# Keys of the first head group by key tiles, another order in the first batch's second pass, and one load of queries moved behind five eighths of w_in

## The chip, the cores and the metric

The kernel runs on one core of a Trainium2 chip. The metric is the time of one execution on the device in microseconds: 383.92 is the median of three runs of the kernel before (383.72 to 384.61).

## What is computed

Sigmoid attention, and a dense layer pair behind it. In float32 the reference is

```
scores = q @ k^T / sqrt(64) - log(448)          # 8 batches, 12 heads, 448 x 64 each
attn   = sigmoid(scores)                        # no softmax
x      = attn @ v, heads side by side           # 3584 tokens x 768
h      = x @ w_in                               # 768 -> 2048
g      = h * sigmoid(beta * h)                  # beta: one number for each of 2048 columns
out    = g @ w_out                              # 2048 -> 768
```

## The kernel before

Everything is multiplied in float16. A batch has three groups of four heads (`QPB` = 3), 24 groups in all. A group is two slots of two heads. The 448 keys of a head are three key tiles of 128 (`jt` 0 to 2) and a last one of 64 (`jt` 3, `JF`); in the raw layout the four blocks of 32 that make up a key tile lie three blocks apart (`(i j) d`, i = 4, j = 3).

**Loads.** POOL issues all loads that cast to float16: queries and keys (`load_one`, L110), values (`load_v`, four loads of 144 KB at L131 and two of 48 KB at L138 for a batch), w_in in eight slices of 256 columns (`load_w_in`, L148), w_out in four (L156). It has eight of them under way: each waits for the one that was issued eight before. SP issues the first group's queries (first half, seven of fourteen blocks) and keys without a cast (L517), as whole float32 rows into `gt`, a tile that is free then, and `beta_in` (L546); later it issues the stores. The order on POOL at the start is: first-half queries and keys of groups 1 and 2, values of batch 0, second-half queries of groups 0, 1 and 2, the eight slices of w_in, queries and keys of group 3, half of w_out, values of batch 1 and so on.

**Transposes.** For group 0, DVE casts the queries (L537), ACT one half of the keys (L539) and DVE the other (L540). DVE transposes queries (L191) and keys (L199 for key tiles 0 to 2 in one instruction, L203 for the last tile).

**The order** of the start is written by hand, under a manual schedule: an engine runs its instructions in the order of the program. The first batch is worked in two passes of 224 queries (`QH`). In the first pass each group has two half visits. The first (`half_visit(g, 0, 0)`) makes the scores of key tiles 0 and 1, the second (`second` = 1) those of tile 2 and of the last one; ACT turns each score tile into attention (L224). Between them PE runs matmuls on zeros (`idle_units`, L533), nine at the very start and then four or two at a time. `attend(g, c0, n)` multiplies attention by values (L279), and DVE copies the result to `xT` (L288). After the first pass comes group 0's second half, in between the attends of the first pass.

Then the fill begins. `fill_units(n)` takes the next n pieces of dense work from a list: for the first 224 tokens sixteen units of the first layer (`dense1`, units 0 to 15; unit dc needs w_in's slice dc // 2), the same for the second 224, with pieces of the second layer between them from the tenth unit on. A unit of the first layer is six matmuls (L166), a sigmoid on ACT (L305) and a product on DVE (L308), which frees its bank; four banks are shared by these units, the attends and the second layer. Around the change the order is

```
        fill_units(4)
        for g in range(1, QPB):
            for second in range(2):
                half_visit(g, QH, second)
                if second:
                    attend(g - 1, QH, QH)
                fill_units(g if second else 2 + g)
        fill_units(1)
        attend(QPB - 1, QH, QH)
```

so units 0 to 3 stand first, 4 to 6 after group 1's first half visit, 7 after its second and attend(0), 8 to 11 after group 2's first, 12 to 14 after its second and attend(1), and 15 after attend(2).

From group 3 on, a planner hands out fill by a budget in microseconds (`M1H_US`, `M2_US` and so on are its costs): after each `visit(g, jt)` it takes units until the budget of that visit is spent. A visit makes the scores of one key tile for the group's two slots and has ACT weigh both.

Of the kernel before, what the change touches and what calls it, by code (L numbers as in the profile page):

```python
# [8 lines left out]
FP32 = mybir.dt.float32  # L9
FP16 = mybir.dt.float16  # L10
# [3 lines left out]
def kernel(  # L14
# [10 lines left out]
    nc = tc.nc  # L25
# [3 lines left out]
    B, H, S, D = q.shape  # L29
    NTOK, DM = out.shape  # L30
    DFF = moe_w_in.shape[1]
    P = 128
    BLK = 32
# [112 lines left out]
    def load_w_in(c: int):  # L146
        n = DFF // WCH
        nc.gpsimd.dma_start(  # L148
            out=w_in16[:, :, c * n : (c + 1) * n],
            in_=moe_w_in[:, c * n : (c + 1) * n].rearrange("(c p) f -> p c f", p=P),  # L150
        )
# [34 lines left out]
    def transpose(g: int, r: int, c0: int = 0, c1: int = NB):  # L186
        raw = raws[g][:, r]
        if r == 0:
            if g not in qT:
                qT[g] = qTp.tile([P, NB * BLK, PAIR], FP16, tag="qT", name="qT")  # L190
            nc.vector.transpose(  # L191
                out=in_order(g // QPB, qT[g][:, c0 * BLK : c1 * BLK]),
                in_=raw[:, c0:c1].rearrange("p c d -> p (c d)").bitcast(FP32),
            )
            return
        kT[g] = kTp.tile([P, S, PAIR], FP16, tag="kT", name="kT")
        to = kT[g].rearrange("p k e -> p (k e)").bitcast(FP32)
        frm = raw.rearrange("p c d -> p (c d)").bitcast(FP32).rearrange("p (c f) -> p c f", c=NB)
        nc.vector.transpose(  # L199
            out=to[:, 0 : JF * P].rearrange("p (j i q) -> p i j q", j=JF, i=HQ),  # L200
            in_=frm[:, 0:NF].rearrange("p (i j) f -> p i j f", j=JF),
        )
        nc.vector.transpose(  # L203
            out=to[:, JF * P :], in_=frm[:, NF:].rearrange("p c f -> p (c f)")
        )

    def score_tile():
# [23 lines left out]
        return at  # L231


    def visit(g: int, jt: int, also=()):
        if jt < JF:
            todo = [(score_tile(), [s]) for s in (2 * g, 2 * g + 1)]
        else:
            todo = [(score_tile(), [2 * h, 2 * h + 1]) for h in (g, *also)]
        for e in range(PAIR):
            for sco, slots in todo:  # L240
                for s in slots:
                    for hh in range(2):
                        score(sco, 0, s, jt, hh, e, 0, S)
        for sco, slots in todo:
            at = weigh(sco, S)
            for s in slots:
                at_tiles[s, jt, 0] = at
# [259 lines left out]
    with tc.manual_schedule():  # L507
        raws[0] = rawp.tile([P, 2, NB, D], FP16, tag="raw", name="raw")
        wide = gt.rearrange("p a b -> p (a b)").bitcast(FP32)
        cut = NH * D  # L510
        early = [(0, 0, NH), (1, 0, NB)]
        staged = {}
        at = 0
        for r, c0, c1 in early:
            staged[r] = wide[:, at : at + (c1 - c0) * D]
            at += (c1 - c0) * D
            nc.sync.dma_start(  # L517
                out=staged[r],
                in_=(q, k)[r][0, 0:HQ].rearrange("h (p c) d -> (h p) (c d)", c=NB)[
                    :, c0 * D : c1 * D  # L520
                ],
            )
        nc.gpsimd.memset(dummy, 0.0)  # L523
        nc.scalar.activation(out=dummy, in_=dummy, func=AF.Sigmoid, bias=0.0, scale=1.0)

# [7 lines left out]
                nc.tensor.matmul(idle, still[:, 0:P], still, start=True, stop=True)  # L533

        idle_units(9)
        raw = raws[0].rearrange("p r c d -> p r (c d)")
        nc.vector.tensor_copy(out=raw[:, 0, 0:cut], in_=staged[0])  # L537
        transpose(0, 0, 0, NH)
        nc.scalar.copy(out=raw[:, 1, cut:], in_=staged[1][:, cut:])  # L539
        nc.vector.tensor_copy(out=raw[:, 1, 0:cut], in_=staged[1][:, 0:cut])  # L540
        transpose(0, 1)
        for g in range(1, QPB):
            load_one(g, 0, 0, NH)
            load_one(g, 1)
        load_v(0)
        nc.sync.dma_start(out=beta_in[0:NDC], in_=moe_beta.rearrange("(c p) -> c p", p=P))  # L546
        for g in range(QPB):
            load_one(g, 0, NH, NB)
        for c in range(WCH):
            load_w_in(c)  # L550
        for g in range(1, QPB):
            transpose(g, 0, 0, NH)
# [10 lines left out]
        half_visit(0, QH, 0)  # L563
        attend(1, 0, QH)
        half_visit(0, QH, 1)
        for g in range(1, QPB):
            transpose(g, 0, NH, NB)
        attend(2, 0, QH, (0,))
        attend(2, 0, QH, (1,))
# [12 lines left out]
        firsts.close()  # L582
        share_psum(ctx, 2, 4)
        fill_units(4)
        for g in range(1, QPB):
            for second in range(2):
                half_visit(g, QH, second)
                if second:
                    attend(g - 1, QH, QH)
                fill_units(g if second else 2 + g)  # L590
        fill_units(1)
        attend(QPB - 1, QH, QH)
        fill_units(1)
        transpose(QPB, 0)
        transpose(QPB, 1)
# [24 lines left out]
        for i, (g, jt, also) in enumerate(visits):  # L620
            if jt == 0:
# [10 lines left out]
                        load_qk(g + 2)  # L632
                if g + 1 < NQUAD and (g + 1) % QPB == 0:
                    load_v((g + 1) // QPB)
            visit(g, jt, also)
            if jt in (1, 2) and QPB < g < NQUAD - 1:
                transpose(g + 1, jt - 1)
            if jt == 2 and g % QPB == 0 and g > QPB:
# [51 lines left out]
```

## Time and profile before

| what | value |
|---|---|
| median of three runs | 383.92 us |
| the profiled execution | 383.76 us |
| its span, first to last instruction | 382.0 us |
| PE busy | 375.9 us, 98% |
| DVE, ACT, POOL busy | 231.8, 229.5, 66.4 us |
| granted clock of PE | 1.00 in all slices |
| keys of group 0, SP's load | 448 KB, 3.3 us to landing |
| first-half queries of group 0, SP's load | 224 KB, 2.7 us to landing |
| one slice of w_in, POOL's load | 384 KB, median 10.7 us to landing |

The span is what the profiler saw between the first and the last instruction; the execution's own time is 1.8 us longer. Sizes of POOL's loads are those of the float16 written; twice as much is read. PE, LDWEIGHTS (PEld), DVE, ACT, POOL and SP are the engines, `L213` is line 213 of the kernel before. Starts in the timeline are microseconds from the first instruction.

### The profile page before, as it was taken

To read this page: it belongs to the slowest core of one execution; us is meant where nothing else is said; L and a number is where in the kernel's file an instruction comes from. 1 tells how busy PE (TensorE), PEld (TensorE's weight loads), DVE (VectorE), ACT (ScalarE), POOL (GpSimd) and SP (SyncE) were. 2 spreads that over 40 slices of the span, in tenths; PEclk is the share of its full clock that TensorE was granted. 3 is DMA by queue.
4 is the path that set the end of the run, shared out by engine and by line. 5 is a ranking of instruction groups with operands and counts; after the bars stand their busy time and mean duration, and the time that the engine had idled before them with its cause. 6 is when DMAs were issued, how large, how long until landed. Compare 5 with 4: busy or idle time off the path is not lost.

```text
span 382.0 us, 8227 instructions
## 1 busy us (share of the span) xinstructions
PE 375.9 (98%) x3415; PEld 199.2 (52%) x3415; DVE 231.8 (61%) x439; ACT 229.5 (60%) x330; POOL 66.4 (17%) x114
## 2 busy tenths in 40 slices
PE   8999999999999999999999999999999999999996
PEld 3478754444654445444554445544456444555563
DVE  3447366775765557555775657665676665655761
ACT  5987856697465786487355782477752787435200
POOL 7833343140110410040110410113100000000000
PEclk9999999999999999999999999999999999999999
DMA  9999999845363930563363750649303300030033
GB/s 165 172 196 204 198 205 209 178 65 59 50 132 83 122 51 2 130 90 32 50 132 84 102 69 2 131 88 118 50 0 84 85 1 2 2 82 0 2 82 125
DMA packets 42405, 34.71 MB, mean 91 GB/s; under 512 B 21872, under 2 KB 38656, under 8 KB 42368
## 3 DMA queue, kind: packets, MB, share of 16 engines
q0 software_dynamic: 36688, 22.47, 43.5%
q1 hardware_dynamic: 5680, 11.71, 11.6%
q8 instruction: 27, 0.44, 0.5%
q14 instruction: 10, 0.08, 0.1%
HBM read 45.62 MB, written 11.01 MB: 148 GB/s over the span
## 4 chain that ended last, share of the span: by engine, by line
PE 92%; DMA 4%; POOL 1%; issue 1%; ACT 0%; DVE 0%; ACTq 0%; POOLq 0%
PE m_ps L166 73%; PE sco L213 10%; PE av_ps L279 9%; DMA w_in<-in_moe_w_in_dram 3%; DMA raw<-in_k_dram 2%; POOL raw L110 1%; POOL w_in L148 1%; ACT attnT L224 0%; ACT sg L305 0%; DVE osb L340 0%; DVE gt L308 0%; POOL dummy L523 0%; ACTq L305 0%; POOLq L674 0%
## 5 line engine op out<-in xcount | busy, mean ns | idle before, releaser
L224 ACT ACTIVATE attnT<-sco 128x896 f16<-128x896 f32 (+1 forms) x171 | 145.2, 902 | 81.1 <-PE sco L213 80.5
L166 PE MATMUL m_ps<-xT,w_in 128*128 128x448 f16 (+2 forms) x1014 | 154.7, 336 | 0.7 <-DMA w_in<-in_moe_w_in_dram 0.5
L308 DVE TENSOR_TENSOR gt<-m_ps,sg 128x448 f16<-128x448 f32 (+1 forms) x144 | 81.4, 572 | 81.6 <-ACT sg L305 78.1
L166 PEld LDWEIGHTS <-w_in 128*128 128x128 f16 (+1 forms) x1014 | 82.8, 101 | 69.3 <-issue 15.1
L305 ACT ACTIVATE sg<-m_ps,beta_sb 128x448 f32<-128x448 f32 (+1 forms) x144 | 84.3, 597 | 36.9 <-PE m_ps L166 29.8
L166 PEld LDWEIGHTS <-sum 128*64 128x64 f16 (+1 forms) x664 | 48.1, 104 | 33.5 <-issue 7.9
L213 PE MATMUL sco<-qT,kT 32*128 32x448 f16 (+3 forms) x864 | 52.0, 341 | 0.7 <-DVE kT L199 0.5
L166 PE MATMUL m_ps<-w_T,sum 128*128 128x384 f16 (+1 forms) x360 | 51.6, 327 | 0.0
L110 POOL DMA_DIRECT2D raw<-in_q_dram x26 | 14.4, 553 | 181.0 <-DVE kT L203 175.5
L428 DVE TENSOR_TENSOR osb<-m_ps,osb 128x384 f32<-128x384 f32 x60 | 33.3, 555 | 18.8 <-PE m_ps L166 16.9
L166 PEld LDWEIGHTS <-gt 128*128 128x128 f16 (+1 forms) x414 | 31.4, 103 | 23.8 <-issue 6.2
L279 PE MATMUL av_ps<-attnT,v 128*64 128x448 f16 (+3 forms) x432 | 40.2, 338 | 0.0
L398 DVE TENSOR_TENSOR sum<-gt 128x1024 f16<-128x1024 f16 x60 | 39.1, 677 | 0.1
L288 DVE CAST xT<-av_ps 128x448 f16<-128x448 f32 (+1 forms) x54 | 28.5, 567 | 15.3 <-PE av_ps L279 14.3
L166 PE MATMUL m_ps<-w_T,gt 128*64 128x384 f16 (+1 forms) x268 | 34.3, 327 | 0.0
L166 PE MATMUL m_ps<-w_out,sum 128*64 128x384 f16 (+1 forms) x304 | 33.8, 327 | 0.0
L279 PEld LDWEIGHTS <-v 128*64 128x64 f16 (+1 forms) x432 | 20.6, 108 | 18.8 <-issue 9.2
L213 PEld LDWEIGHTS <-kT 32*128 32x128 f16 (+1 forms) x864 | 13.7, 96 | 28.6 <-issue 25.7
L166 PE MATMUL m_ps<-w_out,gt 128*128 128x384 f16 (+3 forms) x146 | 22.6, 327 | 0.0
L131 POOL DMA_DIRECT2D v<-in_v_dram x32 | 19.8, 632 | 10.4 <-DMA w_in<-in_moe_w_in_dram 5.6
L191 DVE STREAM_TRANSPOSE qT<-raw 128x448 f32<-128x448 f32 (+1 forms) x27 | 16.6, 616 | 0.4 <-DMA raw<-in_q_dram 0.3
L431 ACT COPY osb<-m_ps 128x384 f32<-128x384 f32 x12 | 5.8, 481 | 16.8 <-PE m_ps L166 16.8
(25 smaller groups left out, 90.1 us busy)
## 6 DMA issues: line engine op xcount, KB each, us to landing
out_dram<-osb SPq DMA_DIRECT2D x98, 96.0 KB, 1.9
raw<-in_k_dram POOLq DMA_DIRECT2D x23, 224.0 KB, 5.3
raw<-in_q_dram POOLq DMA_DIRECT2D x21, 224.0 KB, 3.9
v<-in_v_dram POOLq DMA_DIRECT2D x32, 144.0 KB, 6.5
w_in<-in_moe_w_in_dram POOLq DMA_DIRECT2D x8, 384.0 KB, 10.7
w_out<-in_moe_w_out_dram POOLq DMA_DIRECT2D x4, 768.0 KB, 13.8
v<-in_v_dram POOLq DMA_DIRECT2D x16, 48.0 KB, 5.9
out_dram<-osb SPq DMA_DIRECT2D x2, 384.0 KB, 3.0
```

Of the source, the lines that this page charges most:

```text
L110: nc.gpsimd.dma_start(out=raws[g][:, r, c0:c1].rearrange("p c d -> p (c d)"), in_=(q, k)[r][b, HQ * t : HQ * (t + 1)].rearrange("h (p c) d ...
L131: nc.gpsimd.dma_start(out=vs[b][i * BLK : (i + 1) * BLK, :, 0:JF].rearrange("p h j d -> p h (j d)"), in_=rows[:, :, JF * i * D : JF * (i + ...
L166: nc.tensor.matmul(to[c : c + step], hidden[:, c : c + step], weights, **({} if step == P else {"tile_position": (0, c)}), **flags,)
L191: nc.vector.transpose(out=in_order(g // QPB, qT[g][:, c0 * BLK : c1 * BLK]), in_=raw[:, c0:c1].rearrange("p c d -> p (c d)").bitcast(FP32),)
L213: nc.tensor.matmul(sco[base : base + nk, hh, u0 : u0 + n], kT[g][lo : lo + BLK, jt * P : jt * P + nk, e], qT[g][lo : lo + BLK, c0 : c0 + n ...
L224: nc.scalar.activation(out=at[:, :, 0:n], in_=sco[:, :, 0:n], func=AF.Sigmoid, bias=NEG_LOG_S, scale=MSCALE,)
L279: nc.tensor.matmul(av[hh * D : (hh + 1) * D, 0:n], vs[b][base : base + nk, 2 * (s % NPAIR) + hh, jt], at[base : base + nk, hh, 0:n], start ...
L288: nc.vector.tensor_copy(out=xTs[b][:, s % NPAIR, c0 : c0 + n], in_=av[:, 0:n])
L305: nc.scalar.activation(out=sg[:, 0:n], in_=m1[:, 0:n], func=AF.Sigmoid, bias=0.0, scale=beta_sb[:, dc : dc + 1])
L308: nc.vector.tensor_tensor(out=gt[:, dc, off : off + n], in0=m1[:, 0:n], in1=sg[:, 0:n], op=ALU.mult)
L398: nc.vector.tensor_tensor(out=sums[t, i], in0=x, in1=y, op=op)
L428: nc.vector.tensor_tensor(out=out, in0=in0, in1=in1, op=op)
```

## The change

1. The keys of group 0 come in three loads on SP, behind the queries: key tiles 0 and 1 (per partition four runs of 512 bytes), key tile 2 (four runs of 256 bytes) and the last tile (one run of 512 bytes). Before it was one load with one run of 3584 bytes per partition. ACT casts key tile 1, DVE tile 0; DVE transposes tiles 0 and 1; then DVE casts tile 2 and the last tile, and transposes these two. A new function `transpose_keys(g, j0, j1)` transposes a range of key tiles; for all other groups it is called with the ranges that were used before.
2. The second-half queries of group 2 are loaded behind five of w_in's eight slices, and transposed between the products of units 6 and 7 instead of before attend(2) of the first pass.
3. The second pass of the first batch is written out in another order: attend(0) stands behind group 1's first half visit, attend(1) behind group 2's first, and the units are 4 to 6, 7 to 9, 10 to 12, 13 and 14, and 15.
4. In the third visit that the planner sees (`i == 2`, group 3, key tile 2) one unit is issued between the two sigmoids of the visit, and counted as spent.

```
+    def transpose_keys(g: int, j0: int, j1: int):
+        if g not in kT:
+            kT[g] = kTp.tile([P, S, PAIR], FP16, tag="kT", name="kT")
         to = kT[g].rearrange("p k e -> p (k e)").bitcast(FP32)
+        frm = raws[g][:, 1].rearrange("p c d -> p (c d)").bitcast(FP32)
+        frm = frm.rearrange("p (c f) -> p c f", c=NB)
+        if j0 == JF:
+            nc.vector.transpose(
+                out=to[:, JF * P :], in_=frm[:, NF:].rearrange("p c f -> p (c f)")
+            )
+            return
         nc.vector.transpose(
+            out=to[:, j0 * P : j1 * P].rearrange("p (j i q) -> p i j q", i=HQ, q=BLK),
+            in_=frm[:, 0:NF].rearrange("p (i j) f -> p i j f", j=JF)[:, :, j0:j1],
         )
...
-    def visit(g: int, jt: int, also=()):
+    def visit(g: int, jt: int, also=(), between=None):
...
-        for sco, slots in todo:
+        for x, (sco, slots) in enumerate(todo):
+            if x and between:
+                between()
             at = weigh(sco, S)
...
+        def by_tile(t, j0: int, j1: int):
+            return t[:, 0:NF].rearrange("p (i j) d -> p i (j d)", j=JF)[:, :, j0 * D : j1 * D]
+
+        nc.sync.dma_start(out=q0, in_=q0_in[:, 0:NH])
+        nc.sync.dma_start(out=by_tile(k0, 0, 2), in_=by_tile(k0_in, 0, 2))
+        nc.sync.dma_start(out=by_tile(k0, 2, JF), in_=by_tile(k0_in, 2, JF))
+        nc.sync.dma_start(out=k0[:, NF:], in_=k0_in[:, NF:])
...
-        nc.scalar.copy(out=raw[:, 1, cut:], in_=staged[1][:, cut:])
-        nc.vector.tensor_copy(out=raw[:, 1, 0:cut], in_=staged[1][:, 0:cut])
-        transpose(0, 1)
+        nc.scalar.copy(out=by_tile(raw_k, 1, 2), in_=by_tile(k0, 1, 2))
+        nc.vector.tensor_copy(out=by_tile(raw_k, 0, 1), in_=by_tile(k0, 0, 1))
+        transpose_keys(0, 0, 2)
+        nc.vector.tensor_copy(out=by_tile(raw_k, 2, JF), in_=by_tile(k0, 2, JF))
+        nc.vector.tensor_copy(out=raw_k[:, NF:], in_=k0[:, NF:])
+        transpose_keys(0, 2, JF)
+        transpose_keys(0, JF, JF + 1)
...
-        for g in range(QPB):
+        for g in range(QPB - 1):
             load_one(g, 0, NH, NB)
         for c in range(WCH):
+            if c == WCH // 2 + 1:
+                load_one(QPB - 1, 0, NH, NB)
             load_w_in(c)
...
-        for g in range(1, QPB):
-            for second in range(2):
-                half_visit(g, QH, second)
-                if second:
-                    attend(g - 1, QH, QH)
-                fill_units(g if second else 2 + g)
-        fill_units(1)
-        attend(QPB - 1, QH, QH)
+        half_visit(1, QH, 0)
+        attend(0, QH, QH)
+        fill_units(3)
+        half_visit(1, QH, 1)
+        transpose(2, 0, NH, NB)
+        fill_units(3)
+        half_visit(2, QH, 0)
+        attend(1, QH, QH)
+        fill_units(3)
+        half_visit(2, QH, 1)
+        fill_units(2)
+        attend(2, QH, QH)
         fill_units(1)
...
-            visit(g, jt, also)
+            visit(g, jt, also, (lambda: fill_units(1)) if i == 2 else None)
...
+            if i == 2:
+                spent += M1H_US
```

More of the change, by code (lines that the diff above doesn't have):

```diff
@@ L195, in transpose @@
             return
-        kT[g] = kTp.tile([P, S, PAIR], FP16, tag="kT", name="kT")
-        to = kT[g].rearrange("p k e -> p (k e)").bitcast(FP32)
[L198 to L204, printed above, removed]
+        transpose_keys(g, 0, JF)
+        transpose_keys(g, JF, JF + 1)
+    def transpose_keys(g: int, j0: int, j1: int):
+        if g not in kT:
+            kT[g] = kTp.tile([P, S, PAIR], FP16, tag="kT", name="kT")
+        to = kT[g].rearrange("p k e -> p (k e)").bitcast(FP32)
+        frm = raws[g][:, 1].rearrange("p c d -> p (c d)").bitcast(FP32)
[5 more added lines that the diff above has]
+            return
+        nc.vector.transpose(
+            out=to[:, j0 * P : j1 * P].rearrange("p (j i q) -> p i j q", i=HQ, q=BLK),
+            in_=frm[:, 0:NF].rearrange("p (i j) f -> p i j f", j=JF)[:, :, j0:j1],
         )
@@ L509 @@
         wide = gt.rearrange("p a b -> p (a b)").bitcast(FP32)
[L510 to L522, printed above, removed]
+        k0 = wide[:, 0 : NB * D].rearrange("p (c d) -> p c d", c=NB)
+        q0 = wide[:, NB * D : (NB + NH) * D].rearrange("p (c d) -> p c d", c=NH)
+        k0_in = k[0, 0:HQ].rearrange("h (p c) d -> (h p) c d", c=NB)
+        q0_in = q[0, 0:HQ].rearrange("h (p c) d -> (h p) c d", c=NB)
+        def by_tile(t, j0: int, j1: int):
[4 more added lines that the diff above has]
+        nc.sync.dma_start(out=k0[:, NF:], in_=k0_in[:, NF:])
         nc.gpsimd.memset(dummy, 0.0)
@@ L535 @@
         idle_units(9)
-        raw = raws[0].rearrange("p r c d -> p r (c d)")
-        nc.vector.tensor_copy(out=raw[:, 0, 0:cut], in_=staged[0])
+        raw_q, raw_k = raws[0][:, 0], raws[0][:, 1]
+        nc.vector.tensor_copy(out=raw_q[:, 0:NH], in_=q0)
         transpose(0, 0, 0, NH)
-        nc.scalar.copy(out=raw[:, 1, cut:], in_=staged[1][:, cut:])
-        nc.vector.tensor_copy(out=raw[:, 1, 0:cut], in_=staged[1][:, 0:cut])
-        transpose(0, 1)
+        nc.scalar.copy(out=by_tile(raw_k, 1, 2), in_=by_tile(k0, 1, 2))
[5 more added lines that the diff above has]
+        transpose_keys(0, JF, JF + 1)
         for g in range(1, QPB):
@@ L565 @@
         half_visit(0, QH, 1)
-        for g in range(1, QPB):
+        for g in range(1, QPB - 1):
             transpose(g, 0, NH, NB)
@@ L584 @@
         fill_units(4)
-        for g in range(1, QPB):
-            for second in range(2):
-                half_visit(g, QH, second)
-                if second:
-                    attend(g - 1, QH, QH)
-                fill_units(g if second else 2 + g)
-        fill_units(1)
-        attend(QPB - 1, QH, QH)
+        half_visit(1, QH, 0)
[10 more added lines that the diff above has]
+        attend(2, QH, QH)
         fill_units(1)
```

## The prediction

> **What bounds the kernel now.** I read the page's busy shares first (PE 375.9 of 382.0 us), then PE's waits, to see where the missing 6.1 us lie:
>
> ```profile
> PE idle_ps L533 <- DVE still L527: 1.2, 1, 1.2
> PE sco L213 <- DVE kT L199: 0.5, 1, 0.5
> PE m_ps L166 <- DMA w_in<-in_moe_w_in_dram: 0.5, 1, 0.5
> PE sco L213 <- ACT attnT L224: 0.2, 1, 0.2
> PE m_ps L166 <- DVE gt L308: 0.2, 1, 0.2
> ```
>
> That is 2.6 us; the other 3.5 us stand after the last matmul (last copy and store), which the change does not touch. So nothing but the first 50 us can change. The chain of waits, limited to that part, says what leads up to it:
>
> ```profile
> 2.97 7.01 DMA raw<-in_k_dram
> ...
> 11.55 2.45 POOL w_in L148 x3
> 14.00 9.96 DMA w_in<-in_moe_w_in_dram
> ...
> 24.01 0.75 PE m_ps L166 x6
> ...
> 47.09 0.40 DVE gt L308
> ```
>
> Up to 24.0 us the chain is loading, not arithmetic: the stream of POOL's DMAs, which ends in a slice of w_in. After 24.0 us it is PE. The timeline (start, length, engine, line, last in brackets the idle time before and its releaser) shows both sides, first the engines:
>
> ```profile
> 4.52 0.47 DVE L540 CAST raw<-gt 128x448 f16<-128x448 f32 x1 [0.25 <-DMA gt<-in_k_dram]
> 5.12 0.58 DVE L199 STREAM_TRANSPOSE kT<-raw 128x384 f32<-128x384 f32 x1
> 5.75 0.86 PE L213 MATMUL sco<-qT,kT 32*128 32x224 f16 x16 [0.54 <-DVE kT L199]
> ...
> 14.04 0.69 PE L213 MATMUL sco<-qT,kT 32*128 32x224 f16 x14 [0.18 <-ACT attnT L224]
> 24.01 0.75 PE L166 MATMUL m_ps<-xT,w_in 128*128 128x224 f16 x6 [0.52 <-DMA w_in<-in_moe_w_in_dram]
> 31.38 1.90 PE L166 MATMUL m_ps<-xT,w_in 128*128 128x224 f16 x18
> 47.54 1.31 PE L166 MATMUL m_ps<-xT,w_in 128*128 128x224 f16 x12 [0.17 <-DVE gt L308]
> ```
>
> ```profile
> 26.59 0.62 POOL L131 DMA_DIRECT2D v<-in_v_dram  x1 [1.46 <-DMA w_in<-in_moe_w_in_dram]
> 28.65 0.61 POOL L131 DMA_DIRECT2D v<-in_v_dram  x1 [1.44 <-DMA w_in<-in_moe_w_in_dram]
> 30.64 0.61 POOL L131 DMA_DIRECT2D v<-in_v_dram  x1 [1.37 <-DMA w_in<-in_moe_w_in_dram]
> 32.58 0.61 POOL L131 DMA_DIRECT2D v<-in_v_dram  x1 [1.33 <-DMA w_in<-in_moe_w_in_dram]
> ```
>
> The second fence, of POOL alone, is the key. POOL has eight loads under way and starts the next when the one eight back has landed, so its restarts date the landings of w_in's slices. PE's row at 24.01 and POOL's restart at 24.25 have the same cause, so a landing is 0.24 us before POOL's row: slices 0 to 7 land at about 17.8, 20.0, 22.0, 24.0, 26.35, 28.4, 30.4 and 32.34 us, one in 2.0 us. A slice feeds two units of the first dense layer. Unit 14, the first of slice 7, is the third of the eighteen matmuls' units at 31.38: it starts at 31.38 + 12 x 0.102 = 32.60. **PE is there only 0.26 us behind the data.** Whatever makes PE earlier by more meets slice 7.
>
> **The change, part by part.** PE's list holds the same instructions as before, so every gain is a wait that goes.
>
> *Keys by tiles.* Rows: K's load lands at 4.5 (issue 1.18, 3.3 us to landing), ACT casts half (564 ns), DVE half (472), transposes 128x384 (567), scores at 5.75. The first piece has 4/7 of the bytes. The packet records have K's data between 2.65 and 4.03 us, so its piece ends about 3.4 to 3.5 and lands, with K's own 0.5 us behind the last packet, at about 4.0 (at worst 4.5, as now). Then ACT's cast of 256 columns: the sigmoids of 448 and 896 columns (538 and 915 ns) give 0.84 ns a column, so 564 - 192 x 0.84 = 403 ns. DVE's, after its query work that ends at 4.27, about 0.3; the transpose of 256, between the rows of 224 (395) and 384 (567), 0.43. Scores at 5.05 to 5.35, but the nine idle matmuls fill PE to 5.21. So ACT, which is busy without a gap from 6.65 to 16.1, and behind it PE at 14.04, move forward 0.4 to 0.5 us. Call this x. The casts and transposes of tile 2 and the tail (one more cast and transpose than before, 0.2 to 0.3 us each) lie on DVE between 5.3 and 8, where it idles 1.5 us before 8.04; the second half of group 0's scores needs them by about 7.1. SP issues two more DMAs at 0.42 us; beta_in behind them is read at 19.6. The values arrive no earlier (DVE's copy of their last tile runs 13.87 to 14.22, the first attend reads it at 14.66), which leaves room for x = 0.44.
>
> *Queries of group 2 behind five slices.* 112 KB at w_in's 384 KB in 2.0 us is 0.58 us: slices 0 to 4 land 0.58 earlier, the queries at 25.77 + 0.58 = 26.35, slices 5 to 7 where they were. On POOL the waits eight back shift by one load, with at least six loads still in the queue: hidden. DVE's transpose (0.4) now stands in its queue before unit 7's product and waits for 26.35; behind it wait the products of units 7 to 9 and the copies of attend(1). PE wants none of it before 27.9 (next paragraph); the cover ends if the queries come 1.1 us later.
>
> *The new order, on PE's clock without x.* Units take 0.615 (2.47 for four), score halves 0.51 and 0.63, an attend 0.92, all from the rows around. From 19.19: four units to 21.65, scores of group 1 to 22.16, attend(0) to 23.08, units 4 and 5, unit 6 at 24.3 (slice 3 at 23.4: the 0.52 stall goes), scores 24.9, units 7 to 9 from 25.55 (slice 4 at 25.77, wanted 26.15) to 27.4, scores of group 2 to 27.9, attend(1) to 28.8, units 10 and 11 (slice 5 at 28.4) to 30.0. Unit 12 now wants slice 6 at 30.0, and it lands at 30.4: **a new wait of 0.4**. Then unit 12, scores and unit 13 to 32.25, and unit 14 waits for slice 7, 32.34. Against 32.60 the gain is 0.26. With x, PE only waits longer at units 12 and 14: **the head start is worth nothing there**, unless the stream itself comes earlier. Behind unit 14 the sigmoids of units 13 and 14 queue on ACT after group 2's last scores (915 + 538); by the rows the last copy of attend(2) ends about 35.0, wanted 35.1, so 0 to 0.2 may be lost; I take 0. The later loads have room: group 3's keys are transposed at 36.92 for scores at 37.11, w_out's second load frees POOL at 42.74 for matmuls near 43.1.
>
> *A unit between the two sigmoids of visit 2.* At 45.0 ACT runs two sigmoids of 0.87 before unit 10's, which holds its bank and PE by 0.17 at 47.54. One sigmoid fewer in front releases it 0.87 earlier: 0.17 gained. The delayed attention tile is wanted after 49.
>
> *What the small pieces do to the stream.* This is the open price, and it passes one for one to slice 7. No row has 256- or 512-byte loads on SP's queue in number. Packet records of that queue: 1792 bytes 74 ns, 3584 bytes 140 ns, stores of 1024 and 2048 bytes 45 and 83; a line through them gives 27 ns at 512 and 17.5 at 256. On each of 16 engines K is now 32 + 32 + 8 packets: 0.86 + 0.56 + 0.22 = 1.64 us against 8 x 140 = 1.12, so +0.52. beta_in's few 512-byte packets took 40 ns; at that 72 x 40 = 2.88, +1.76, the upper end. POOL's queue speaks for less:
>
> ```profile
> 4.80:6.00 1.20, 0.66 (x9) 0.21 (x12) 0.90 (x3) 0.29 (x1) 1.19 (x2) 1.00 0.84 113
> 9.40:11.00 1.60, 1.60 (x28) 0.69 (x25) 0.70 (x2) 1.46 (x3) 0.81 (x3) 1.00 1.59 188
> 11.60:12.40 0.80, 0.80 (x4) 0.20 (x2) 0.00 (x0) 0.80 (x2) 0.80 (x2) 1.00 1.87 173
> ```
>
> The last two columns are the DMA engines' busy share and GB/s written. In 9.4 to 11.0 values in 768-byte packets run at 188, in 11.6 to 12.4 mostly 256-byte packets at 173: 8% less, 0.1 us on K's 1.1. And from 4.8 to 6.0 the stream starts slowly, 113 GB/s at a share of 0.84, so that pieces of K falling there cost little, or, if POOL's loads begin between them, nothing: the slow start lasts 1.2 us at 0.6 of the later rate, so 0.5 to 0.6 could be won, the lower end. I take +0.2: the line's 0.52, as the same queue's rows are nearest, less what the idle share covers.
>
> **Sum.** -0.26 + 0.2 - 0.17 = -0.23 us. The profiled execution took 383.76 (span 382.0 and 1.8 around it), 0.16 under the median of 383.92: 383.53, or 383.69 from the median. I predict **383.6 us**: no change by the 0.2% (0.77 us) that a measurement of this kernel can tell.
>
> **Rivals.**
> *The stream gains* (faster). POOL's first load is issued at 1.27 but its data starts at 3.75, when K is through; if it gets in between K's pieces, K's rest rides in the slow start. Slice 7 at 31.75, PE with x ready at 31.65: 0.85 + 0.17 = 1.02 gained, 382.7. For it: the share of 0.84. Against: more packets. It needs a stream 0.35 earlier.
> *Small packets are dear* (slower). At 40 ns slice 7 comes at 34.1: +1.76 - 0.26 - 0.17 = +1.33, 385.1. For it beta_in's packets, against it the 256-byte window. It decides above +1.2 us.
> *K's pieces wait their turn* (slower). beta_in, issued 1.65 behind K, landed 5.1 us later at 6.75, 2.3 us after K: a DMA of SP's queue stands behind POOL's loads. So tile 2 would come after group 1's first queries and the tail after group 1's keys, whose data ended near 6.6: landing about 7.5. Casts and transposes (0.7) and scores put ACT's third sigmoid at L + 1.55 against 8.38 now. PE had 0.52 + 0.17 of waits to lose, so a loss of 0.77 needs L above 8.3; at 9.5 the price is 2.67 - 0.71 = +1.96, 385.7. [...]
> That the first piece lands no earlier than K did is part of the main case, since x is worth nothing.
>
> **Numbers.** Main case 0.53: the stream between -0.35 and +1.2, 383.1 to 384.7 counted from the median. Stream gains 0.27. Dear packets 0.10, late pieces 0.10. So faster 0.27, same 0.53, slower 0.20. The range takes in the first two rivals' ends, as both are bounds of the one unknown price, and leaves out the third: 382.6 to 385.1.
>
> **What would show it.** Scores first at 5.2 to 5.4, ACT's gapless run from about 6.2; no wait of PE at unit 6; waits for w_in at units 12 and 14; slice 7 (POOL's fourth restart) at 32.6 to 32.8 instead of 32.58; no wait at 47.5. I am wrong if slice 7 moves by more than 0.4 either way, if ACT has gaps between 6 and 16, or if PE waits for a product or a copy near 35.

## The result, and the profile after

The changed kernel takes 386.32 us (median of 22 executions, 383.81 to 388.41), the kernel before, run beside it, 383.90 (22 executions, 383.07 to 385.20). The ratio is 1.0052 with a 95% interval of 1.0035 to 1.0068: slower by 1.3 to 2.6 us. The forecast of 383.6 us was wrong, and 386.32 lies above its range.

The profiled execution is no help at first sight: it took 383.81 us with a span of 382.0, the same span as before. It is the shortest of the 22. Sorted by the mean granted clock that each execution's record gives, the 22 fall into three groups that do not overlap:

| mean granted clock of PE | executions | time, us | median, us |
|---|---|---|---|
| 0.999 to 1.000 | 7 | 383.81 to 385.08 | 384.34 |
| 0.994 to 0.996 | 10 | 385.74 to 386.93 | 386.35 |
| 0.989 to 0.991 | 5 | 387.26 to 388.41 | 387.78 |

So two things have to be found: what costs some 0.4 us at full clock (384.34 against 383.90), and what lowers the clock in 15 of 22 executions. The first can be traced from the page of the first group, if it is read closely, and it points at the second. Here are PE's waits after (us in total, times, longest):

```profile
PE sco L221 <- DVE kT L210: 1.5, 1, 1.5
PE idle_ps L542 <- DVE still L536: 1.2, 1, 1.2
PE sco L221 <- ACT attnT L232: 0.2, 1, 0.2
```

The 0.5 us for w_in and the 0.2 for DVE's product are gone, as the change meant. (For w_in that says little by itself: a kernel below with the old order of the second pass, the keys alone, does not wait for w_in either, because its PE comes late.) The wait for group 0's keys has grown from 0.5 to 1.5 us. The chain of waits up to 55 us (start, length, what) says which keys:

```profile
2.19 5.88 DMA gt<-in_k_dram
8.10 0.23 DVE raw L552
8.32 0.23 DVE kT L210
...
8.60 0.70 PE sco L221 x16
...
20.24 2.47 PE m_ps L166 x24
```

Before, the chain ran through POOL's loads to a slice of w_in at 24.0 us and met PE only there. Now it is one DMA of SP's queue: the load of the last key tile, 64 KB, issued at 2.19 and landed at 8.10. The whole of K, 448 KB, took 3.3 us in the kernel before. The timeline after (start, length, engine, line, last in brackets the idle time before and its releaser) has the rest:

```profile
4.30 0.29 DVE L549 CAST raw<-gt 128x256 f16<-128x256 f32 x1
5.24 0.86 PE L221 MATMUL sco<-qT,kT 32*128 32x224 f16 x16
6.95 0.29 DVE L551 CAST raw<-gt 128x256 f16<-128x256 f32 x1 [1.77 <-DMA gt<-in_k_dram]
8.10 0.23 DVE L552 CAST raw<-gt 128x128 f16<-128x128 f32 x1 [0.85 <-DMA gt<-in_k_dram]
8.60 0.70 PE L221 MATMUL sco<-qT,kT 32*128 32x224 f16 x16 [1.54 <-DVE kT L210]
9.35 7.78 ACT L232 ACTIVATE attnT<-sco 128x896 f16<-128x896 f32 x10 [1.50 <-PE sco L221]
20.17 2.53 PE L166 MATMUL m_ps<-xT,w_in 128*128 128x224 f16 x24
29.79 1.90 PE L166 MATMUL m_ps<-xT,w_in 128*128 128x224 f16 x18
31.85 0.61 POOL L131 DMA_DIRECT2D v<-in_v_dram  x1 [1.44 <-DMA w_in<-in_moe_w_in_dram]
45.29 3.72 PE L166 MATMUL m_ps<-xT,w_in 128*128 128x224 f16 x36
```

The rows of the kernel before that belong beside the two at 8.60 and 20.17 are

```profile
7.52 0.80 PE L213 MATMUL sco<-qT,kT 32*128 32x224 f16 x16
19.19 2.53 PE L166 MATMUL m_ps<-xT,w_in 128*128 128x224 f16 x24
```

The first scores start at 5.24, as forecast (5.75 before). Tile 2 lands at 6.95 and the last tile at 8.10, the second half of the scores starts at 8.60 (7.52 before), and the first dense unit, which stood at 19.19, at 20.17: **PE enters the dense work 0.98 us later instead of 0.5 earlier.** From there on it waits for nothing (the 18 matmuls at 29.79 and the 36 at 45.29 run through), so the rest takes 382.0 - 20.17 = 361.8 us instead of 362.8, and the two differences cancel. POOL's restart at 31.85 stood at 32.58: the stream of loads came 0.73 us earlier. In windows of the profile (us, then busy times by engine, then clock, DMA share, GB/s) the slow start that the prediction pointed at is gone; the first of its three windows had a DMA share of 0.84 and 113 GB/s:

```profile
4.80:6.00 1.20, 1.18 (x17) 0.44 (x16) 0.38 (x1) 0.00 (x0) 1.20 (x3) 1.00 1.05 173
9.40:11.00 1.60, 1.60 (x21) 0.72 (x20) 1.10 (x5) 1.46 (x3) 0.91 (x2) 1.00 1.59 188
```

### The profile page after: what moved, and what is told of

It reads as the page before. It is cut to its first block, busy times and chain, and to the rows that moved or that the text cites. A ratio compares the mean times of both kernels' runs of the same rounds, so it can differ in the third digit from the quotient of the medians.

```text
span 382.0 us, 8234 instructions
## 1 busy us (share of the span) xinstructions
PE 375.7 (98%) x3415; PEld 199.3 (52%) x3415; DVE 232.1 (61%) x442; ACT 229.1 (60%) x330; POOL 66.5 (17%) x114
## 4 chain that ended last, share of the span: by engine, by line
PE 96%; DMA 2%; ACT 0%; SPq 0%; DVE 0%; issue 0%; ACTq 0%
PE m_ps L166 74%; PE sco L221 12%; PE av_ps L289 9%; DMA gt<-in_k_dram 2%; PE idle_ps L542 1%; ACT attnT L232 0%; SPq L530 0%; DVE osb L350 0%; SPq L529 0%; DVE gt L318 0%; SPq L528 0%; ACT sg L315 0%; DVE kT L210 0%; DVE raw L552 0%; ACTq L315 0%
```

## The experiments

All are edits of the changed kernel, compared with the kernel before on the same chip (medians of 383.4 to 383.7 there). The table collects the results; "scores" is the start of the second half of group 0's scores and "dense" that of the first dense unit, both in the profiled execution, and "rest" is its span less "dense".

| kernel | median, us | ratio to before (95%) | mean clock | scores | dense | rest |
|---|---|---|---|---|---|---|
| before (its first profile) | 383.90 | | 1.000 | 7.52 | 19.19 | 362.8 |
| changed (its first profile) | 386.32 | 1.0052 (1.0035 to 1.0068) | 0.989 to 1.000 | 8.60 | 20.17 | 361.8 |
| keys alone | 386.67 | 1.0080 (1.0052 to 1.0108) | 0.991 to 0.996 | 10.72 | 24.43 | 362.1 |
| keys as before | 383.26 | 0.9992 (0.9973 to 1.0011) | 0.998 to 1.000 | 7.37 | 19.04 | 362.4 |
| the same again | 383.10 | 0.9981 (0.9959 to 1.0003) | 0.998 to 1.000 | 7.65 | 19.23 | 362.7 |
| pause filled | 384.94 | 1.0036 (1.0018 to 1.0053) | 0.999 to 1.000 | 10.36 | 21.93 | 361.9 |
| changed, again | 386.65 (one execution) | | 0.996 | 10.07 | 23.02 | 361.9 |
| one load, small runs | 387.50 | 1.0098 (1.0061 to 1.0135) | 0.991 to 0.999 | 11.48 | 23.16 | 361.9 |
| three loads, large runs | 386.19 | 1.0069 (1.0047 to 1.0090) | 0.991 to 1.000 | 10.55 | 22.50 | 361.9 |
| POOL begins later | 383.86 | 1.0003 (0.9986 to 1.0021) | 0.999 to 1.000 | 7.16 | 18.73 | 362.8 |
| pieces on ACT's queue | 383.83 | 0.9998 (0.9981 to 1.0016) | 0.998 to 1.000 | 7.80 | 19.46 | 361.8 |
| small runs, POOL later | 385.17 | 1.0017 (0.9991 to 1.0043) | 0.996 to 1.000 | 7.96 | 19.62 | 362.1 |
| queries on ACT's queue | 383.48 | 0.9985 (0.9963 to 1.0007) | 0.998 to 1.000 | 7.54 | 19.12 | 363.5 |
| rest in long runs | 387.05 | 1.0102 (1.0085 to 1.0119) | 0.991 to 0.996 | 9.97 | 22.98 | 361.9 |

The last column carries the reading of all others, with one profiled execution for each kernel. From the first dense unit on, a kernel with the new order takes 361.8 to 361.9 us (362.1 in one) when PE has no wait for w_in, however late it starts; only the kernels that are early enough to wait for w_in (0.2 to 1.1 us) take more. **In these executions the time is decided before the dense work begins**, and of that by two columns: when the second half of the scores starts, and how long it is from there to the dense work, 11.6 us at full clock. (With one and three loads the pause lies ahead of the first scores, so that "scores" holds a part of what the clock costs there.)

The kernel before is not free of a low clock either: of its 92 executions beside the experiments, six had a mean clock of 0.994 to 0.996 and took 385.1 to 386.7 us. None of the six was profiled, so what lowered it there is not known.

### Which part does it: the keys alone, and everything but the keys

```
-        for g in range(QPB - 1):
+        for g in range(QPB):
             load_one(g, 0, NH, NB)
...
-            if c == WCH // 2 + 1:
-                load_one(QPB - 1, 0, NH, NB)
...
-        half_visit(1, QH, 0)
-        attend(0, QH, QH)
...
+        for g in range(1, QPB):
+            for second in range(2):
+                half_visit(g, QH, second)
...
-            visit(g, jt, also, (lambda: fill_units(1)) if i == 2 else None)
+            visit(g, jt, also)
```

> Only the keys of group 0 by key tiles (part 1) on the kernel before; order, queries of group 2 and visit 2 as before. Theory A, K's last pieces come late, PE pauses about 1.5 us near 7 to 8.6 us, and in most executions the granted clock falls after the pause: waits of PE at scores near 8.6, median 386.0 to 386.8, mean clock 0.989 to 0.996 in most executions. Without the clock it would be +0.98 (late scores) - 0.52 (no wait for w_in) = +0.46, 384.4. Theory B, the new order of the second pass or the later queries cost the time: at most 384.4, clock 1.00.

The counterpart has part 1 taken back and the other three kept:

```
-        nc.sync.dma_start(out=by_tile(k0, 0, 2), in_=by_tile(k0_in, 0, 2))
-        nc.sync.dma_start(out=by_tile(k0, 2, JF), in_=by_tile(k0_in, 2, JF))
-        nc.sync.dma_start(out=k0[:, NF:], in_=k0_in[:, NF:])
+        nc.sync.dma_start(out=k0, in_=k0_in)
...
+        nc.scalar.copy(out=raw_k[:, NH:], in_=k0[:, NH:])
+        nc.vector.tensor_copy(out=raw_k[:, 0:NH], in_=k0[:, 0:NH])
+        transpose(0, 1)
```

> The changed kernel with K in one load, cast and transposed as before; parts 2 to 4 stay. Theory A: no pause near 8 us, clock 1.00 in all executions, and the working of the prediction without its price of small packets holds: -0.26 (slice 7 of w_in at 32.3) - 0.17 (visit 2) = -0.43, 383.3 to 383.6, ratio 0.9985 to 0.9995. Theory B: 385.5 to 386.5, as the changed kernel.

Measured: 386.67 us for the keys alone (7 executions, ratio 1.0080), 383.26 for the rest without them (12 executions, 0.9992). **The loss is in part 1.** In the keys-alone kernel the last tile landed at 10.22 us, not 8.10. PE's longest wait and the windows of PE (us, PE busy, clock, DMA share, GB/s) show what came of it:

```profile
PE sco L221 <- DVE kT L210: 3.8, 1, 3.8
```

```profile
7.00:8.00 1.00, 0.00 (x0) 1.00 1.19 206
8.00:9.00 1.00, 0.00 (x0) 1.00 1.31 200
9.00:10.00 1.00, 0.00 (x0) 0.51 1.50 191
10.00:11.00 1.00, 0.28 (x8) 0.50 1.58 187
...
13.00:14.00 1.00, 1.00 (x14) 0.50 1.33 179
14.00:16.00 2.00, 2.00 (x16) 0.54 0.94 110
16.00:18.00 2.00, 2.00 (x32) 1.00 1.39 178
```

PE stands idle from 6.94 to 10.72, and the granted clock falls to a half while it does. It stays there until about 15.8: (1 - 0.54) / 0.5 x 2 = 1.84 us of the window from 14 to 16. From the scores to the dense work it is then 13.7 us instead of 11.6. Of the 5.24 us by which the dense work starts later than before, 3.2 are the late keys (10.72 against 7.52) and the other 2.0 to 2.1 the clock.

Everything but the keys behaves as the prediction had it. The new wait for w_in, forecast as 0.4 us at unit 12, is there (0.25 us here, 0.50 in the repetition), and nothing waits at 47.5:

```profile
30.22 0.75 PE L166 MATMUL m_ps<-xT,w_in 128*128 128x224 f16 x6 [0.25 <-DMA w_in<-in_moe_w_in_dram]
```

Whether these parts gain anything is a matter of 0.4 us, so the kernel was run again with 12 more executions.

> Parts 2 to 4 without the keys by tiles, once more on the chip and in the rounds of the run beside it, to narrow the interval: by the two gains named in the prediction 0.9985 to 0.9995; if the gain was chance, 1.000.

It gave 383.10 us, 0.9981 (0.9959 to 1.0003). The two results weighed by the inverse of their variances give about 0.9987 (0.9973 to 1.0002): in the direction of the forecast 0.43 us (0.26 and 0.17, a ratio of 0.9989), and not separated from no change.

### How much of it is the clock

PE has no other work between the two halves of group 0's scores while it waits for the keys, so more idle matmuls there shorten the pause without moving a load:

```
-                    idle_units(4 if g < QPB - 1 else 2)
+                    idle_units(11 if g + second == 0 else 4 if g < QPB - 1 else 2)
```

> The changed kernel with eleven instead of four idle matmuls between the two half visits of group 0: seven more of 0.216 us fill the 1.5 us in which PE waits for K's tile 2. The scores come no earlier. Theory A: clock 1.00 in all executions and the time of the changed kernel's executions at full clock, 383.8 to 384.5, ratio 1.000 to 1.001. Rival, the late scores themselves make the 2.4 us by what they delay: the time stays at 386 to 386.6.

Beside it the changed kernel itself was profiled again:

> The changed kernel once more, for a profile of an execution whose mean clock is below 1. Theory A: the granted clock is low in one stretch that begins within some 4 us of the pause at 7 to 8.6 us, and matmuls take up to twice their time there, nowhere else. Rival: the low stretch lies somewhere else in the kernel, and the pause has nothing to do with it.

With the pause filled the clock was 0.999 or 1.000 in all twelve executions, where it had fallen in 15 of 22 of the changed kernel; the pause was 1.99 us in the profiled one, as the row at 10.36 below shows. But the time was 384.94 us, 1.0036 of before, more than I had expected. The timeline of PE says why: seven more matmuls cover 1.5 us, and the keys came later than that.

```profile
5.83 2.55 PE L542 MATMUL idle_ps<-still 128*128 128x512 f16 x11
10.36 0.70 PE L221 MATMUL sco<-qT,kT 32*128 32x224 f16 x16 [1.99 <-DVE kT L210]
```

So the delay is a cost of its own, 1.3 us of the median (384.94 against 383.64), and what the changed kernel loses beyond it, 2.4 - 1.3 = about 1.1 us, goes with the clock. That is an estimate from the medians of two separate measurements; by the ratios, 1.0052 against 1.0036, it would be 0.6 us, and their intervals overlap. The second profile of the changed kernel, at 386.65 us, has both. Its tile 2 landed at 9.36 instead of 6.95, PE waited 2.29 us, and its row and the windows of PE read:

```profile
10.07 0.76 PE L221 MATMUL sco<-qT,kT 32*128 32x224 f16 x16 [2.29 <-DVE kT L210]
```

```profile
8.00:9.00 1.00, 0.00 (x0) 1.00 1.45 189
9.00:10.00 1.00, 0.00 (x0) 1.00 1.56 191
10.00:11.00 1.00, 0.93 (x17) 0.79 1.60 187
11.00:12.00 1.00, 1.00 (x3) 0.50 1.91 174
...
13.00:14.00 1.00, 1.00 (x14) 0.51 0.89 106
14.00:16.00 2.00, 2.00 (x24) 1.00 1.09 137
```

PE has work again from 10.07 on, and the clock falls all the same, at about 10.58, for 0.42 + 2 + 0.98 = 3.40 us. From the scores to the dense work it takes 12.95 us where the pause-filled kernel takes 11.57: 1.38 us for one such stretch. The keys-alone kernel's stretch is 6.8 us, twice as long. Two stretch lengths fit the groups of the first table: 1 - 0.5 x 3.4 / 386 is a mean clock of 0.996, and 1 - 0.5 x 6.8 / 386 is 0.991.

What separates the pauses that cost the clock from the others can be read from the clock records of the traces. The clock's changes within one profile lie whole multiples of 3.41 us apart (375.47 us, 110 times 3.413, in the first profiles of both kernels; 3.40 and 6.8 us above), and the first of them comes at 3.88 to 7.16 us, at another place in every profile. So these profiles read as if the clock went by windows of 3.41 us whose place differs from one execution to the next. What PE's matmuls fill of the window that holds the pause separates the two outcomes in all profiles with a pause above 1.5 us:

| profile | window, us | PE busy, us | clock behind it |
|---|---|---|---|
| pause filled | 8.90 to 12.31 | 1.95 (57%) | full |
| changed (first profile) | 5.89 to 9.30 | 1.87 (55%) | full |
| keys alone | 5.60 to 9.02 | 1.35 (39%) | half |
| changed, again | 7.16 to 10.57 | 1.13 (33%) | half |
| rest in long runs | 7.29 to 10.70 | 0.73 (21%) | half |
| three loads, large runs | 4.78 to 8.19 | 0.47 (14%) | half |
| one load, small runs | 4.94 to 8.35 | 0.20 (6%) | half |

In four of the five profiles with half clock it lasted one window, and PE was busy for 87% (one load) to 100% of that window. Only in the keys-alone kernel it lasted two: in the window from 9.02 to 12.43 PE was busy for half of the time, in the next one for all of it.

The lengths of 3.40 and 6.8 us agree with one and two such windows, and a window whose place differs from one execution to the next would explain why the same kernel falls into three groups. The window did not have to be idle: 39% of busy time was still too little here, and 55% was enough.

### Why the pieces land late: how many loads, or how large their runs

Two things set the pieces apart from the one load of before: they are issued over 1.0 us more (at 1.18, 1.64 and 2.19), so that POOL's loads (the first issued at 1.27, its first packet at 3.35 in the first profile) are under way before the later ones are (tile 2's first packet there at 3.84), and they are moved in runs of 256 and 512 bytes instead of 3584. Each can be had without the other. One load with runs of 512 bytes (in the staging tile 128 bytes are left between the pairs of blocks, so that the runs stay apart):

```
-        nc.sync.dma_start(out=by_tile(k0, 0, 2), in_=by_tile(k0_in, 0, 2))
...
+        k0 = wide[:, 0 : NH * 160].rearrange("p (x r) -> p x r", r=160)[:, :, 0 : 2 * D]
+        nc.sync.dma_start(out=k0, in_=k0_in.rearrange("p (x c) d -> p x (c d)", c=2))
...
+        transpose(0, 1)
```

> As the kernel with K in one load (parts 2 to 4 kept), but that one load is cut into runs of 512 bytes by gaps in the staging tile: 7 packets per partition in place of 1. It tells packet size from the number of loads. Theory A (a load of SP's queue that stands behind POOL's loads waits for them): one load keeps its place, the packets take 27 ns each, 56 on each DMA engine, 1.5 us against 1.12, so K lands about 4.9 instead of 4.5, scores at 6.1, no wait of PE over 1.2 us, clock 1.00, 383.2 to 383.9. Theory C (small packets lose against POOL's larger ones): K lands at 7 or later, a pause of PE of over 2 us, a low clock, 386 or more.

Three loads with runs of 2048, 1024 and 512 bytes (8, 4 and 2 blocks); here the first scores need two of them:

```
+        for c0, c1 in ((0, 8), (8, NF), (NF, NB)):
+            nc.sync.dma_start(out=k0[:, c0:c1], in_=k0_in[:, c0:c1])
...
+        transpose_keys(0, 0, JF)
...
```

> K in three loads again, of 8, 4 and 2 blocks, each one contiguous run per partition of 2048, 1024 and 512 bytes, cast when they land; the transposes of key tiles 0 to 2 need the first two. Theory A: the second load lands only after POOL's first loads, at 6.5 to 9.5, though its packets are large; the first scores start at 7.5 to 10, PE pauses 2 us or more from 5.2, mean clock below 1, 386 to 389. Theory C: all three land by 4.8, scores at 6, clock 1.00, 383.2 to 383.9.

And the changed kernel with POOL's first load put off by a memset of a part of `gt` that nothing reads:

```
         nc.gpsimd.memset(dummy, 0.0)
+        nc.gpsimd.memset(wide[:, 4096:6144], 0.0)
```

> The changed kernel with a memset of 2048 columns on POOL in front of its first load (into a part of a tile that is written later), so that POOL's loads begin 1 to 2 us later and K's pieces are all in the queue by then. Theory A: tile 2 lands at about 4.6 to 5.2, the last piece by 5.7, no pause of PE over 0.5 us behind 6 us, clock 1.00; the price is the stream of loads, 0.3 to 1 us later at slice 7, so 384.0 to 385.0. Theory C: tile 2 still lands late and the clock still falls, 386 or more.

Neither of the first two came in time. The one load landed at 7.61 us instead of 4.5, the three at 4.04, 6.96 and 8.37, and both lose about as much as the changed kernel or more (1.0098 and 1.0069 against 1.0052; the intervals of the last two overlap). From the timelines of the one load and of the three:

```profile
7.61 0.43 DVE L548 CAST raw<-gt 128x512 f16<-128x512 f32 x1 [3.37 <-DMA gt<-in_k_dram]
```

```profile
6.96 0.29 DVE L548 CAST raw<-gt 128x256 f16<-128x256 f32 x1 [2.65 <-DMA gt<-in_k_dram]
8.37 0.23 DVE L550 CAST raw<-gt 128x128 f16<-128x128 f32 x1 [0.43 <-DMA gt<-in_k_dram]
```

So the small runs are not needed for a late landing: the second piece has runs of 1024 bytes and lands at 6.96 as tile 2 did at 6.95. But the idea that one load keeps its place in line fell too: with runs of 512 bytes it did not. Its packets take longer to issue (SP 0.69 us instead of 0.42) and begin at 3.00 us, 0.27 after POOL's first at 2.73, so that the two run beside each other from there on. What both have in common is that POOL's loads are under way beside the pieces (the first issued at 1.26 in both), and the third run moves those. With POOL's first load at 2.51 instead of 1.27 the changed kernel's tile 2 lands at 6.29, and the last tile by 6.67 (expected were 4.6 to 5.2 and 5.7, so they still lose time on the way):

```profile
0.77 1.80 POOL L533 MEMSET gt<- 128x2048 f32 x1
2.51 0.67 POOL L110 DMA_DIRECT2D raw<-in_q_dram  x1
```

```profile
6.29 0.47 DVE L552 CAST raw<-gt 128x256 f16<-128x256 f32 x1 [1.13 <-DMA gt<-in_k_dram]
7.16 0.70 PE L221 MATMUL sco<-qT,kT 32*128 32x224 f16 x16 [0.40 <-DVE kT L210]
30.37 0.75 PE L166 MATMUL m_ps<-xT,w_in 128*128 128x224 f16 x6 [0.50 <-DMA w_in<-in_moe_w_in_dram]
```

PE's pause is 0.4 us, the clock full in all ten executions and the time 383.86, 1.0003 of before. The same three pieces of the same small runs cost nothing when POOL's loads begin 1.24 us later. What is won ahead of the dense work (18.73 against 19.19) is lost at w_in, which this stream brings no earlier: 0.50 us at unit 12, as the prediction said of a head start.

The same memset in front of the one load with small runs was to check this from the other side.

> K in one load of 512-byte runs (7 packets per partition), now with the 1.80 us memset on POOL in front of its first load. The one load of small runs came at 7.6 though it was one load: its first packet started at 3.0, behind POOL's first at 2.73. Theory A mended (what counts is whether POOL's loads are in line when K's packets come up; small runs take SP longer to issue, 0.69 against 0.42, and give POOL's loads more turns): without POOL in line K lands at about 4.8 to 5.2, no pause of PE over 1.5 us, clock 1.00, 383.3 to 384.3. Rival (56 small packets on each engine are slow by themselves): K lands at 6.5 or later, and the clock falls.

Its keys landed at 5.30 instead of 7.61, close to the 4.8 to 5.2 expected and as turns with POOL's loads would have it. Its time, 385.17 (383.43 to 386.39), missed the expected 383.3 to 384.3 and is not explained: the profiled execution, at 383.43, is the shortest, the mean clock is 0.998 or more in nine of ten, and the others are up to 3 us longer.

The packet records, which say when each piece of a load was moved, show how a late load ends. In the second profile of the changed kernel half of tile 2's 512 packets of 256 bytes start by 4.68 us and 90% by 6.77; the landing waits for the last 24, which come in evenly spaced steps: 0.161 us apart up to 7.94, then 0.095, and 0.014 at the end, where 18 ns is what such a packet takes. Each step is the time of one packet of POOL's loads (154 or 88 ns there) and 7 ns more. That reads as **one packet of K, one of POOL's** (the records name no DMA engine; that the tail belongs to one is read from the even steps): the last 24 packets take 1.7 us where alone, at 18 ns each, they would take 0.4. In the first profile, with tile 2 at 6.95, no such steps show: its last 24 packets start at most 0.015 us apart. If one packet goes for one, fewer and longer packets must land sooner, which was tested by replacing the last two pieces by a load of all of K in runs of 3584 bytes, eight for each of the 16 DMA engines:

```
-        nc.sync.dma_start(out=by_tile(k0, 2, JF), in_=by_tile(k0_in, 2, JF))
-        nc.sync.dma_start(out=k0[:, NF:], in_=k0_in[:, NF:])
+        k1 = wide[:, 2048 : 2048 + NB * D].rearrange("p (c d) -> p c d", c=NB)
+        nc.sync.dma_start(out=k1, in_=k0_in)
...
+        nc.vector.tensor_copy(out=by_tile(raw_k, 2, JF), in_=by_tile(k1, 2, JF))
+        nc.vector.tensor_copy(out=raw_k[:, NF:], in_=k1[:, NF:])
```

> The changed kernel, but tile 2 and the last piece come out of one second load of all of K, one run of 3584 bytes per partition into a place of its own: 448 KB instead of 192 KB behind tiles 0 and 1, in 8 packets on each DMA engine instead of 32 + 8. In the trace of the changed kernel taken again the last 256-byte packets stand 0.16 and then 0.095 us apart, the time of one packet of POOL's between two of K's. Theory A sharpened (the engine gives the queues turns packet by packet): 8 turns of 0.154 and 8 packets of 0.14 are 2.4 us from about 3.7, so it lands at 6.2 to 7.0 although it has more bytes; a pause of PE of at most 1.2 us, clock 1.00 in most executions, 384 to 385. Rival (turns by bytes, or the number of loads alone): 448 KB take longer than 192, landing at 9 or later, 386 to 388.

It did not: the load landed at 9.27, and the time is 387.05 (1.0102). Both are what the rival in the expectation named, 9 or later and 386 to 388.

```profile
9.27 0.29 DVE L551 CAST raw<-gt 128x256 f16<-128x256 f32 x1 [4.05 <-DMA gt<-in_k_dram]
9.97 0.70 PE L221 MATMUL sco<-qT,kT 32*128 32x224 f16 x16 [3.16 <-DVE kT L210]
```

A spacing that fits turns is there: the last packets, of 153 ns, start 0.284 us apart, room for one of theirs and one of POOL's. But eight such turns are 2.3 us, and the rest of the delay is that the last of them begin only at 6.4 to 6.7 us, while half of the 128 packets had started by 5.24. So the spacing of these two tails fits turns, but turns do not foretell the landing, and the rival that the number of loads alone delays them is not excluded. Why the last packets begin so much later than the others, and why the landing differs so much from one execution to the next (tile 2 at 6.95, 9.36, 9.38 and 9.66 us in four profiles with the same loads), **stays open**.

### Another queue for the pieces

ACT has no work on the keys before 4.30 us in the changed kernel and can issue loads too, so pieces can be issued earlier (here tile 2 at 0.73 us and the last tile at 1.23, where SP did it at 1.64 and 2.19):

```
-        nc.sync.dma_start(out=by_tile(k0, 2, JF), in_=by_tile(k0_in, 2, JF))
-        nc.sync.dma_start(out=k0[:, NF:], in_=k0_in[:, NF:])
+        nc.scalar.dma_start(out=by_tile(k0, 2, JF), in_=by_tile(k0_in, 2, JF))
+        nc.scalar.dma_start(out=k0[:, NF:], in_=k0_in[:, NF:])
```

> The changed kernel with tile 2 and the last piece of K issued by ACT, ahead of its table load, instead of third and fourth on SP: they are in line about 1 us earlier and ahead of POOL's first load. Theory A: both land by about 5.5, the second half visit starts at 7.1 as forecast, no pause, clock 1.00, and the forecast of the prediction holds: 383.1 to 383.7, ratio 0.998 to 1.000. If the ACT queue shares turns with SP's so that tiles 0 and 1 come later: scores at 5.6 to 6, the same time. Theory C: late as before, 386.

In the other split SP issues tiles 0 and 1 and the last tile, ACT the queries and tile 2:

```
-        nc.sync.dma_start(out=q0, in_=q0_in[:, 0:NH])
         nc.sync.dma_start(out=by_tile(k0, 0, 2), in_=by_tile(k0_in, 0, 2))
-        nc.sync.dma_start(out=by_tile(k0, 2, JF), in_=by_tile(k0_in, 2, JF))
+        nc.scalar.dma_start(out=q0, in_=q0_in[:, 0:NH])
         nc.sync.dma_start(out=k0[:, NF:], in_=k0_in[:, NF:])
+        nc.scalar.dma_start(out=by_tile(k0, 2, JF), in_=by_tile(k0_in, 2, JF))
```

> The changed kernel with group 0's loads on two queues: SP issues tiles 0 and 1 first and then the last piece, ACT the queries and then tile 2, so that all four are in line by about 2.7 us. Theory A: all land by 5.2, scores at 5.2 to 5.8, no pause over 0.7 us, clock 1.00, and the stream of loads not later than in the kernel before; 382.9 to 383.5, which would be the fastest. If four loads in turn all end together near 4.8: scores near 6, 383.3 to 383.8. Theory C: 386.

Both keep the clock (0.998 or more in all 24 executions), and neither beats the kernel before: 383.83 (0.9998) and 383.48 (0.9985, 0.9963 to 1.0007). In the first one tiles 0 and 1 land at 5.38 instead of 4.30 (DVE casts the others at 6.29 and 6.50 without a wait for them), so that the first scores wait until 6.32 and the second follow at 7.80; PE waits for no w_in. In the second one the scores start at 5.61 and 7.54, and PE gives 1.1 us to w_in in two waits. The lowest median of all is that of the kernel with the keys loaded as before, 383.10 to 383.26, and it is not separated from the kernel before either.

## Why the prediction was wrong

**The bound was read rightly.** Nothing but the first 50 us changed. The waits that were to go (0.52 at unit 6, 0.17 at 47.5) are gone in the profile after, and how closely PE runs behind w_in shows in the new wait of the next paragraph.

**Queries behind five slices, the new order, a unit between two sigmoids: right.** The new wait came at unit 12 as named, 0.25 and 0.50 us against 0.4, in the two kernels with the keys as before; the second wait that was named, at unit 14, came in neither. The forecast gain of 0.43 us lies inside what these two measured together, from 1.0 us faster to 0.1 slower.

**Keys by tiles, first scores: right.** 5.24 against 5.05 to 5.35, and tiles 0 and 1 landed at 4.30, between the 4.0 taken and the 4.5 called worst.

**The price of small pieces for the stream: the size of a packet was right, the sign of the sum not.** The line through the records gave 27 ns for 512 bytes and 17.5 for 256; the records of the first profile have 27 and 18 in the median, and 40 and 31 for many of those that POOL's loads run beside. But the stream did not come 0.2 us later in the profiled execution; it came 0.73 earlier, more than the 0.4 that the prediction had named as a sign of being wrong. It looks like the rival "The stream gains", for the slow start carried more (173 GB/s instead of 113 from 4.8 to 6.0), but that mechanism is not shown: from 4 to 6 us both profiles of the changed kernel moved 187 GB/s, and in the second one slice 7 came 1.2 us later than before (POOL's restart at 33.80). In the first profile the gain was worth nothing, since PE was 0.98 us later by then.

**The step that failed is the landing of K's later pieces.** The main case said that the second half of group 0's scores needs them by about 7.1 and let them have it. The rival "K's pieces wait their turn" named what came, a DMA of SP's queue that is late beside POOL's loads (tile 2 at 6.95 to 9.66 with POOL's first load at 1.27, at 6.29 with it at 2.51), and even its price: a loss when the last piece lands after 8.3. I gave it 0.10 because I put the landing at about 7.5, from the end of the data of group 1's keys at 6.6. That estimate lets K's rest through when the loads queued ahead of it have moved. But the tail in the second profile reads as turns (a packet of K in 0.161 us beside POOL's of 154 ns), and the one row that spoke of the time a load takes there, beta_in's 5.1 us for 8 KB, gave 2.2 + 5.1 = 7.3 for a load of very few packets; the last piece has 128 packets, behind tile 2's 512, 8 and 32 for each of 16 engines, and I added nothing for them. Measured: 8.10 in the best profile, about 9.5 to 10.2 in three others with the same loads, and ACT's gap of 1.50 us ahead of 9.35 is the sign that the prediction had named for it. With 9.5 the rival's own sum gave 385.7 (the waits that it takes off are 0.52 + 0.17 = 0.69, not 0.71, which changes nothing in that figure). How much of the delay is turns and how much the late start of the last packets stays open, as said above.

**A term was missing altogether: the granted clock.** It was 1.00 in every slice of the page before, and I took it as given. In the profile of the kernel before no pause of PE between its first matmul and its last is longer than 0.54 us. The pauses of 2.29 to 3.78 us that late keys made left PE at most 39% of a window of 3.41 us, and the clock was halved for 3.4 or 6.8 us, which costs 1.4 to 2.1 us. This is what the rival's sum did not have: of the 2.0 to 2.4 us lost, about 1.3 go with the delay and 0.6 to 1.1 with the clock.

## What to carry to other kernels

When a load is split, price the later pieces by when they are issued against the other queue's loads, and leave room: the same tile 2 landed at 6.95 to 9.66 us in four profiles with POOL's first load at 1.27, and at 6.29 with it at 2.51, and neither its bytes nor its packets foretold it. Before a wait of TensorE is made longer, ask how much of a window of 3.41 us it can leave empty, for here the pauses of 2.29 to 3.78 us, which left PE 6 to 39% of one, cost the clock as well, and those of 1.54 and 1.99, which left it 55 and 57%, did not; fill the pause with idle matmuls or keep it short. And when executions of one kernel fall into groups, look at the granted clock of each first: the profile that one happens to hold may be from the group without the loss.

## What the runs showed that was not expected

- The granted clock fell for stretches of 3.40 us or twice that. It fell after pauses of PE of 2.29 (the changed kernel again), 2.94 (three loads), 3.16 (rest in long runs), 3.65 (one load) and 3.78 us (keys alone), in the pause or up to 0.7 us after PE had begun to work again; not after 1.54 (changed) nor in twelve executions of the pause-filled kernel, whose profiled one had 1.99.
- In the tails of two late loads two DMA queues seem to alternate packet by packet: in the second profile of the changed kernel 256-byte packets, 18 ns each alone, advance one in 0.161 us beside POOL's 154 ns, and in the kernel with the rest in long runs those of 153 ns one in 0.284.
- SP took 0.69 us to issue a load of 896 runs, but the number of runs alone does not set it: tiles 0 and 1, 512 runs, took 0.42, and the last tile, 128 runs, 0.50.
- The start reads as half clock, though the first slices of the page say 1.00. The clock records begin only at 3.88 to 7.16 us (6.42 in the kernel before, 5.89 in the changed one); ahead of that the idle matmuls start 0.427 us apart, later ones 0.216.
- The clock does not explain all of the spread. Of the kernels with one and with three loads, three executions with a mean clock of 0.999 or 1.000 took 387.4 to 387.7 us, as long as those with a lower one. The late landing alone can cost as much; no profile of such an execution was taken.
